# Attention, soft mixture of experts and a Mish layer on one core: the products of probabilities and values in two blocks a pair of heads, and one column block of the folded weights moved ahead of the last layer

## The chip, the cores and the metric

One NeuronCore of one Trainium2 chip runs the program. The metric is device time in microseconds (us) of one execution; the time of a kernel is the median of several runs. Engines: PE is TensorE (PEld its weight loads), DVE VectorE, ACT ScalarE, POOL GpSimd, and SP the queue that issues the DMAs.

## What is computed

```python
# attention: 4 batches, 8 heads, 576 tokens, 64 numbers a head
q_rot, k_rot = rotate(q), rotate(k)
scores = scale * q_rot @ k_rot.T
attn = softmax(scores)                 # over the keys
x = (attn @ v)                         # -> 2304 tokens x 512
# soft mixture of experts, 8 experts of 4 slots
logits = x @ phi                       # 2304 x 32
d = softmax(logits, over tokens); c = softmax(logits, over slots)
slot_out[e] = relu((d.T @ x)[e] @ w1[e]) @ w2[e]
x = c @ slot_out                       # 2304 x 512
# last layer
h = x @ w_in                           # 2304 x 2048
return (h * tanh(softplus(h))) @ w_out # 2304 x 512
```

## The kernel before, in words

**Attention.** The 32 heads are taken as 16 pairs. A pair has nine tiles of scores (128 queries by 576 keys; the ninth holds the last 64 queries of both heads). Each tile goes through four steps: PE multiplies (S, `s_tile`, L333 and L335, or L353 for the ninth), DVE takes the negated row maximum (M, `s_max`, L361), ACT takes the exponential (E, `s_exp`, L367), and PE transposes the 128x128 blocks (T, `t_head`, L374; K, `t_keys`, L388; R, `t_rem`, L394 and L396). ACT or DVE (`evac`, L410 and L413; `t_rem`, L398 to L401) copies the transposed blocks into the tiles PT: group 0 (256 queries: query tiles 0 and 1) and group 1 (320 queries: tiles 2, 3 and the rest).

**Products of probabilities and values.** `av(p, g, c)` (L429) multiplies, for key block c of 0 to 4 and for both heads h, a 128x64 block of values by PT into 64 of the 128 partitions of the PSUM tile `m_av`: head 0 into the lower half, head 1 into the upper half. So a group has ten such products, and a pair has two groups. A product in plain fp32 is two matmul records in the trace. The order in the source is c = 0 head 0, c = 0 head 1, c = 1 head 0 and so on; c = 4 (the last 64 keys, values `vrem`) ends the group, which is then copied out (`xts`) and transposed back (X, `xback`, L449 to L457).

**Order of the work.** The table `PLAN` has one line for each of nine steps of a pair p. A letter is an action, the digit its index, and a "-" behind it means that it is done for pair p - 1. V are the five parts of group 0, W those of group 1. The lines of the table give the order in which the instructions are traced; a scheduler then sets the order of each engine's queue from dependencies and its own model, and may move an instruction ahead of others. `keep_in_program_order` puts an instruction behind the one that was traced before it on its engine. Each engine works through its queue in order.

**Behind the attention** come the routing sums, the experts (L834 and L900, with weights that stream in by DMA), and the last layer. There the product of the slots' outputs with `w_in` is folded: `inner_a(j)` (L981) multiplies the slots' outputs `s_t` with 256 columns of `w_in`, four parts side by side in `m_wp`, and ACT copies them out (L982); `inner_b(j)` (L987) adds the four parts on PE into `m_w`, ACT copies the high part into `wst` (L989) and DVE subtracts to get the low part (L990). `mish(u)` takes unit u (256 tokens, one j): PE makes `hp` from `wst` and the combine weights (L1004), ACT takes Mish (L1011), and the result is split into `gh` and `gl` (L1013, L1019). `second(u)` multiplies both with the parts `wo_h`, `wo_l` of `w_out` into `o_ps` (L1038), 12 products a unit. `parts_of` (L944, L945) and `cv` split `w_out` along the way. `idle(n)` is n products of the identity with itself, whose result is not used (L553). In this part all instructions are pinned to the source's order.

Of the kernel before, what the change touches and what calls it, by code (L numbers as in the profile page):

```python
# [24 lines left out]


PLAN = (
    "L T7- S M K1- E V3- V4-",
    "X0- R- C S M E",
    "S M E W0-",  # L30
    "F T0 r C S M E",
    "S a W1- W2- k F F W3- M T2 T1 E C",
    "S d q C M E",
    "S M C a E T3 W4-",
    "S a C T4 M E",
    "V0 K0 T5 d C F S F M T6 V1 E X1- d V2",
)

EVAC = {"T3": "d", "T4": "d", "K1": "a", "T0": "a", "T5": "a", "T2": "a"}
# [3 lines left out]
def kernel(  # L43
# [13 lines left out]
    nc = tc.nc  # L57
    NB, H, S, D = q.shape
    E, DM, F1 = w1.shape
# [148 lines left out]
    def load_v(p):  # L208
        b, h = divmod(2 * p, H)
        t = vs[p % 3]  # L210
        dma(
            out=t.rearrange("p h c d -> p h (c d)"),
            in_=v[b, h:h + 2, 0:512, :].rearrange("h (p c) d -> p h (c d)", c=4),
        )
        vt[p] = t
# [189 lines left out]
    def evac(dst, src, n, key=None):  # L405

        on = EVAC.get(key) or ("a" if load["a"] <= load["d"] else "d")
        if on == "a":
            load["a"] += n / 1.2 + 50
            nc.scalar.copy(dst, src)  # L410
        else:
            load["d"] += n / 0.96 + 65
            nc.vector.tensor_copy(dst, src)  # L413
# [3 lines left out]
    def av(p, g, c):  # L417
        b, hp = divmod(p, H // 2)
        n = 256 + g * R
        if c == 0:  # L420
            av_ps[p, g] = ps_a.tile([128, n], F32, tag="av", name="m_av")
        ps, pt = av_ps[p, g], PT[p, g]
        for h in range(2):
            o = 64 * h
            if c < 4:
                lhsT, rhs = vt[p][:, h, c, :], pt[:, 5 * h + c, :]
            else:
                lhsT, rhs = vrem[b % 2][:, hp, h, :], pt[:, 4, :]
            nc.tensor.matmul(ps[o:o + 64, :], lhsT=lhsT, rhs=rhs, start=(c == 0), stop=(c == 4))  # L429
        if c == 4:  # L430
            PT.pop((p, g))
            ps = av_ps.pop((p, g))
            xs = a4.tile([128, n], F32, tag="xts", name="xts")
            evac(xs, ps, n, f"X{g}")
            xts[p, g] = xs
            if g and p + 3 < NP:
                load_v(p + 3)
# [111 lines left out]
    def warm(pool, tag, n):  # L549

        ps = pool.tile([128, 128], F32, tag=tag, name="warm")
        for _ in range(n):
            tc.keep_in_program_order(nc.tensor.matmul(ps, lhsT=ident, rhs=ident, start=True, stop=True))  # L553
# [222 lines left out]
    ps = ps_m.tile([128, KDM, NSLOT], F32, tag="m", name="m_sit")  # L776
# [50 lines left out]
    for eg in range(2):  # L827
        for hf in range(2):
            end = eg == 1 and hf == 1
            for fh, cc in [(fh, cc) for fh in range(2) for cc in range(2)]:  # L830
                c = 2 * hf + cc
                for g in range(4):
# [3 lines left out]
                        rhs=parts[1, e, hf][0][:, cc * F1 + fh * 512:cc * F1 + fh * 512 + 512],  # L836
                        start=(eg == 0 and c == 0), stop=(eg == 1 and c == KDM - 1),
# [56 lines left out]
    for eg in range(2):  # L894
        for hf in range(2):
            for cc in range(4):
                c = 4 * hf + cc
                for g in range(4):
# [3 lines left out]
                        rhs=parts[2, e, hf][0][:, cc * DM:(cc + 1) * DM],  # L902
                        start=(eg == 0 and c == 0), stop=(eg == 1 and c == F1 // 128 - 1),
# [8 lines left out]
    ps = ps_m.tile([128, KDM, NSLOT], F32, tag="m", name="m_sot")  # L912
# [28 lines left out]
    def parts_of(c):  # L941

        x = wo_l[c].bitcast(F32)
        pin(nc.scalar.copy(wo_h[c], x))  # L944
        pin(nc.vector.tensor_tensor(out=wo_l[c], in0=x, in1=wo_h[c].bitcast(F32), op=ALU.subtract))  # L945
# [21 lines left out]
    def convert(n):  # L967
        while n:
            x = next(steps2, None)
            if x is None:  # L970
                return
            cv(*x)
            n -= x[1] not in ("S", "H")

    def inner_a(j):

        fb, o = divmod(j * 256, 512)
        wi = parts[3, fb, 0][0].rearrange("p (c f) -> p c f", c=KDM)[:, :, o:o + 256]
        ps = ps_p.tile([128, 256], F32, tag="p", name="m_wp")
        for c in range(KDM):  # L980
            pin(nc.tensor.matmul(ps[32 * c:32 * c + 32, :], lhsT=s_t[:, c, :], rhs=wi[:, c, :], start=True, stop=True))  # L981
        pin(nc.scalar.copy(wps[j % 2], ps))  # L982

    def inner_b(j):

        ps = ps_p.tile([128, 256], F32, tag="p", name="m_w")
        pin(nc.tensor.matmul(ps, lhsT=rr, rhs=wps[j % 2], start=True, stop=True))  # L987
        dst = wst[:, j * 256:(j + 1) * 256]
        pin(nc.scalar.copy(dst, ps))  # L989
        pin(nc.vector.tensor_tensor(out=dst[64:128], in0=ps[64:128], in1=dst[64:128].bitcast(F32), op=ALU.subtract))  # L990
# [3 lines left out]
    NG = NFC // 2  # L994
# [4 lines left out]
    def mish(u):  # L999
        i, j = units[u]  # L1000
        hp = ps_p.tile([128, 2, 256], F32, tag="p", name="hp")
        for x in range(2):
            f = 2 * j + x
            pin(nc.tensor.matmul(hp[:, x, :], lhsT=wst[:, f * 128:(f + 1) * 128],  # L1004
                                 rhs=ct[:, i * 256:(i + 1) * 256],
                                 start=True, stop=True))
        hp = hp.rearrange("p a n -> p (a n)")
        gg = ggs[u % 3]
        gh = p6.tile([128, 512], F32R, tag="gh", name="gh", bufs=LOOK + 1)
        gl = p6.tile([128, 512], F32R, tag="gl", name="gl", bufs=LOOK + 1)  # L1010
        pin(nc.scalar.activation(out=gg, in_=hp, func=AF.Mish))  # L1011

        pin((nc.scalar.copy if 0 < u < NG * GR else nc.vector.tensor_copy)(gh, gg))  # L1013
        gs[u] = gh, gl, gg
# [46 lines left out]
    def idle(n):  # L1061

        warm(ps_o, "o", n)

    inner_a(0)
    parts_of(0)
    idle(3)
    inner_b(0)
    parts_of(1)
    cv(NCE, "S")  # L1070
    idle(6)
    for u in range(len(units) + 2):

        lag = 1 if u < NG * GR else 2
        if u < len(units):
            g, j = units[u][0] // GR, units[u][1]
            i = units[u][0] % GR
            mish(u)
            if u == 0:
                convert(3)  # L1080
                idle(5)
            else:
                if g == 0 or u == NG * GR:
                    rest(u - 1)
                    if u == 1:
                        parts_of(2)
                        parts_of(3)
                    convert(3 + (i == 0))
                if g:
                    rest(u)  # L1090
        else:
            g = None
        if u >= lag and u != NG * GR:
            second(u - lag)
        if g == 0 and i == 2 and j in (0, 2):
            fetch((3, 2 + j // 2, 0), behind=True)
        if g == 0 and j + 1 < NG:

            if i == 0:
                inner_a(j + 1)  # L1100
            elif i == 1:
                inner_b(j + 1)
# [51 lines left out]
```

## Time and profile before

| | us |
|---|---|
| median of 3 runs | 672.29 (671.97 to 673.31) |
| the profiled execution, whole | 671.88 |
| span of its trace | 670.1 |
| attention up to the experts' first product | 0 to 398.8 |
| experts | 398.8 to 434.5 |
| last layer | 434.5 to 670.1 |

The 1.8 us between the whole execution and the span lie around the traced instructions. A row's start is counted from the start of the span. A matmul's end is modelled, so the duration in a row reaches over the start of the next row; what a matmul takes of PE's queue is read from the start of one row to the start of the next.

### The profile page before, as it was taken

What the parts mean: (1) busy time and instruction counts of PE and PEld (TensorE: products, weight loads), DVE (VectorE), ACT (ScalarE), POOL (GpSimd) and SP (SyncE); (2) the same over time, 40 slices, a digit from 0 to 9 for tenths busy, and PEclk for the clock granted to TensorE, in tenths of its full rate; (3) what the DMA queues carried; (4) which work ended last, traced back from release to release, by engine and by line L of the source; (5) the groups of instructions that cost most, each with busy time, mean ns of one, the idle gap of its engine ahead of it and who ended that gap; (6) DMA issues with size and microseconds to landing.
All of it is one profiled execution on the core that took longest, in us unless ns stands there. A gap on an engine that the chain in (4) does not pass through costs nothing.

```text
span 670.1 us, 11089 instructions
## 1 busy us (share of the span) xinstructions
PE 625.2 (93%) x4022; PEld 461.3 (69%) x4022; DVE 406.5 (61%) x824; ACT 336.4 (50%) x757; POOL 218.2 (33%) x263
## 2 busy tenths in 40 slices
PE   1598999989899999999999998999999999999997
PEld 1475677666577767777667653377787888888885
DVE  5777888786686866565756533177876533353342
ACT  2566776684776556665656411167765312222121
POOL 5758869755858644345400010000000000000000
PEclk9999999999999999999999999999999999999999
DMA  9678689868786965346359499962400200030004
GB/s 259 160 187 236 187 268 273 231 212 237 161 266 218 264 184 166 103 128 189 81 176 302 158 338 324 389 262 95 156 33 31 64 1 0 1 95 0 1 1 94
DMA packets 59607, 109.43 MB, mean 163 GB/s; under 512 B 12832, under 2 KB 25248, under 8 KB 59040
## 3 DMA queue, kind: packets, MB, share of 16 engines
q1 hardware_dynamic: 59552, 108.72, 54.2%
q8 instruction: 32, 0.52, 0.3%
q14 instruction: 23, 0.19, 0.1%
HBM read 70.25 MB, written 9.96 MB: 120 GB/s over the span
## 4 chain that ended last, share of the span: by engine, by line
PE 77%; DMA 9%; DVE 7%; ACT 2%; POOL 2%; issue 2%; SPq 1%; DVEq 0%; ACTq 0%; POOLq 0%
PE o_ps L1038 29%; PE m_av L429 13%; PE t L374 7%; PE s L333 5%; PE s L335 4%; PE hp L1004 3%; PE s L353 2%; DMA w<-in_moe_w_in_dram 2%; PE so_ps L900 2%; DMA w<-in_moe_w_dram 2%; DVE nmax L361 1%; PE m_lg L455 1%; PE tk L388 1%; PE m_k L285 1%; DMA w<-in_moe_w_out_dram 1%
## 5 line engine op out<-in xcount | busy, mean ns | idle before, releaser
L361 DVE TENSOR_REDUCE nmax<-s 128x1 f32<-128x576 f32 x144 | 108.0, 753 | 64.3 <-PE s L335 39.5
L367 ACT ACTIVATE P<-s,nmax 128x576 f32<-128x576 f32 x144 | 107.2, 745 | 36.3 <-DVE nmax L361 25.5
L1038 PE MATMUL o_ps<-wo_l,gh 128*128 128x512 f32 x288 | 112.9, 392 | 0.0
L1038 PE MATMUL o_ps<-wo_h,gh 128*128 128x512 f32 x288 | 112.9, 392 | 0.0
L1038 PE MATMUL o_ps<-wo_h,gl 128*128 128x512 f32 x288 | 100.7, 390 | 0.9 <-DVE gl L1019 0.9
L1011 ACT ACTIVATE room<-hp 128x512 f32<-128x512 f32 x72 | 43.0, 599 | 106.7 <-PE hp L1004 102.2
L333 PE MATMUL s<-qk_st 128*128 128x288 f32 x256 | 85.6, 349 | 10.3 <-ACT P L367 5.2
L374 PE MATMUL t<-cs,P 128*128 128x128 f32 x512 | 79.0, 282 | 4.8 <-ACT P L367 2.7
L410 ACT COPY PT<-t 128x512 f32<-128x512 f32 x92 | 53.5, 586 | 49.8 <-PE t L374 49.2
L429 PE MATMUL m_av<-PT,w 128*64 128x320 f32 (+1 forms) x384 | 73.3, 421 | 1.9 <-ACT PT L399 1.3
L374 PEld LDWEIGHTS t<-cs,P 128*128 128x128 f32 x512 | 59.6, 143 | 21.8 <-issue 9.7
L335 PE MATMUL s<-k_st,qk_st 128*128 128x288 f32 x256 | 73.8, 302 | 0.0
L333 PEld LDWEIGHTS s<-qk_st 128*128 128x128 f32 x256 | 49.9, 195 | 29.5 <-ACT P L367 9.1
L1013 DVE CAST gh<-room 128x512 fp32r<-128x512 f32 x49 | 20.9, 427 | 79.4 <-ACT room L1011 79.3
L1038 PEld LDWEIGHTS o_ps<-wo_h,gl 128*128 128x128 f32 x288 | 53.9, 188 | 13.2 <-DVE gl L1019 1.7
L231 POOL TENSOR_TENSOR w<-w,cs 128x512 f32<-128x512 f32 x34 | 45.2, 1332 | 54.1 <-PE m_k L285 46.6
L1038 PEld LDWEIGHTS o_ps<-wo_h,gh 128*128 128x128 f32 x288 | 54.1, 188 | 9.4
L1038 PEld LDWEIGHTS o_ps<-wo_l,gh 128*128 128x128 f32 x288 | 54.3, 189 | 9.0 <-DVE wo_l L891 0.2
L1019 DVE TENSOR_TENSOR gl<-room,gh 128x512 fp32r<-128x512 f32 x72 | 49.6, 691 | 4.6
L335 PEld LDWEIGHTS s<-k_st,qk_st 128*128 128x128 f32 x256 | 50.2, 196 | 0.0
L228 POOL TENSOR_TENSOR w<-w,cs 128x512 f32<-128x512 f32 x34 | 45.7, 1345 | 8.6 <-DMA w<-in_q_dram 2.9
L429 PEld LDWEIGHTS m_av<-PT,w 128*64 128x64 f32 x384 | 26.5, 136 | 23.0 <-issue 9.2
(175 smaller groups left out, 1011.5 us busy)
## 6 DMA issues: line engine op xcount, KB each, us to landing
w<-in_moe_w_dram SPq DMA_DIRECT2D x28, 1024.0 KB, 7.1
w<-in_moe_w_in_dram SPq DMA_DIRECT2D x16, 512.0 KB, 7.3
qk_st<-parth SPq DMA_DIRECT2D x46, 144.0 KB, 3.2
qk_st<-partl SPq DMA_DIRECT2D x46, 144.0 KB, 3.2
room<-in_moe_w_out_dram SPq DMA_DIRECT2D x12, 512.0 KB, 3.6
w<-in_q_dram SPq DMA_DIRECT2D x16, 256.0 KB, 5.2
w<-in_k_dram SPq DMA_DIRECT2D x16, 256.0 KB, 4.6
w<-in_moe_w_dram SPq DMA_DIRECT2D x16, 256.0 KB, 5.6
```

The costliest lines, as they stand in the source:

```text
L228: eng.tensor_tensor(out=tb, in0=src, in1=sin.to_broadcast([128, n, w]), op=ALU.mult)
L231: eng.tensor_tensor(out=dst, in0=sv, in1=cv, op=ALU.mult)
L333: nc.tensor.matmul(s[:, half, 0:288], lhsT=st[:, qc:qc + 128], rhs=st[:, KC + o:KC + o + 288], start=first, stop=False)
L335: nc.tensor.matmul(s[:, half, 0:288], lhsT=st[:, qc:qc + 128], rhs=k2_st[p % 2][:, o:o + 288], start=False, stop=last)
L361: nc.vector.tensor_reduce(out=stat[p][0][:, i:i + 1], in_=s[:, :, 0:288], axis=AX.XY, op=ALU.max, negate=True)
L367: nc.scalar.activation(out=P[p, t][:, h * S:(h + 1) * S].rearrange("p (a b) -> p a b", a=2), in_=s[:, :, 0:288], func=AF.Exp, bias=stat[p] ...
L374: nc.tensor.transpose(ps[:, j, :], P[p, t][:, blk * 128:(blk + 1) * 128], ident)
L410: nc.scalar.copy(dst, src)
L429: nc.tensor.matmul(ps[o:o + 64, :], lhsT=lhsT, rhs=rhs, start=(c == 0), stop=(c == 4))
L1011: pin(nc.scalar.activation(out=gg, in_=hp, func=AF.Mish))
L1019: pin(nc.vector.tensor_tensor(out=gl, in0=gg, in1=gh.bitcast(F32), op=ALU.subtract))
L1038: pin(nc.tensor.matmul(ops[i, n], lhsT=g_[:, cols], rhs=w_[f], start=(j == 0 and (x, k) == (0, 0)), stop=(j == NG - 1 and all(y[0] != n fo ...
```

## The change

All ten products of group 0 (V0 to V4) are traced in step 0 of the next pair, and all ten of group 1 (W0 to W4) in step 4; before, V0 to V2 stood in step 8 of the own pair, and W0 to W4 in steps 2, 4 and 6. Every product but the first of its group is pinned behind the instruction that was traced before it on PE. In the last layer `inner_a(1)` and `inner_b(1)` are moved from inside the first units to the place ahead of the first `mish`, `inner_b(0)` now stands ahead of `parts_of(0)`, and nine `idle` products ahead of the first `hp` become two. The loop makes `inner_a` and `inner_b` for j = 2 to 7.

```diff
@@ -25,15 +25,15 @@
 
 
 PLAN = (
-    "L T7- S M K1- E V3- V4-",
+    "L T7- S M K1- E V0- V1- V2- V3- V4-",
     "X0- R- C S M E",
-    "S M E W0-",
+    "S M E",
     "F T0 r C S M E",
-    "S a W1- W2- k F F W3- M T2 T1 E C",
+    "S a W0- W1- W2- W3- W4- k F F M T2 T1 E C",
     "S d q C M E",
-    "S M C a E T3 W4-",
+    "S M C a E T3",
     "S a C T4 M E",
-    "V0 K0 T5 d C F S F M T6 V1 E X1- d V2",
+    "K0 T5 d C F S F M T6 E X1- d",
 )
 
 EVAC = {"T3": "d", "T4": "d", "K1": "a", "T0": "a", "T5": "a", "T2": "a"}
@@ -426,7 +426,10 @@
                 lhsT, rhs = vt[p][:, h, c, :], pt[:, 5 * h + c, :]
             else:
                 lhsT, rhs = vrem[b % 2][:, hp, h, :], pt[:, 4, :]
-            nc.tensor.matmul(ps[o:o + 64, :], lhsT=lhsT, rhs=rhs, start=(c == 0), stop=(c == 4))
+            mm = nc.tensor.matmul(ps[o:o + 64, :], lhsT=lhsT, rhs=rhs, start=(c == 0), stop=(c == 4))
+            if c or h:
+
+                tc.keep_in_program_order(mm)
         if c == 4:
             PT.pop((p, g))
             ps = av_ps.pop((p, g))
@@ -1063,12 +1066,13 @@
         warm(ps_o, "o", n)
 
     inner_a(0)
+    inner_a(1)
+    inner_b(0)
     parts_of(0)
-    idle(3)
-    inner_b(0)
+    inner_b(1)
     parts_of(1)
     cv(NCE, "S")
-    idle(6)
+    idle(2)
     for u in range(len(units) + 2):
 
         lag = 1 if u < NG * GR else 2
@@ -1094,7 +1098,7 @@
             second(u - lag)
         if g == 0 and i == 2 and j in (0, 2):
             fetch((3, 2 + j // 2, 0), behind=True)
-        if g == 0 and j + 1 < NG:
+        if g == 0 and 0 < j < NG - 1:
 
             if i == 0:
                 inner_a(j + 1)
```

**PE's queue in a pair, group 1 (64x320), before.** S rows are L333 and L335, `t` a transpose, `m_rem` and `m_k` transposes for the next pair.

```order
L374 MATMUL t<-cs,P 128x128 x4
L429 MATMUL m_av<-PT,w_5_1_102 64x320
L333 MATMUL s<-qk_st_123 128x288
L335 MATMUL s<-k_st_121,qk_st_123 128x288
L333 MATMUL s<-qk_st_123 128x288
L335 MATMUL s<-k_st_121,qk_st_123 128x288
L429 MATMUL m_av<-PT,w_5_1_102 64x320
L262 MATMUL m_rem<-cs,w_7_0_100 128x128
L429 MATMUL m_av<-PT,w_5_1_102 64x320 x6
L285 MATMUL m_k<-cs,w_7_0_100 128x128 x4
L429 MATMUL m_av<-PT,w_5_0_98 64x320
L374 MATMUL t<-cs,P 128x128 x4
```

The same place now:

```order
L429 MATMUL m_av<-PT,w_5_1_102 64x320
L333 MATMUL s<-qk_st_123 128x288
L335 MATMUL s<-k_st_121,qk_st_123 128x288
L333 MATMUL s<-qk_st_123 128x288
L335 MATMUL s<-k_st_121,qk_st_123 128x288
L262 MATMUL m_rem<-cs,w_7_0_100 128x128
L429 MATMUL m_av<-PT,w_5_1_102 64x320 x7
L285 MATMUL m_k<-cs,w_7_0_100 128x128 x4
L429 MATMUL m_av<-PT,w_5_0_98 64x320 x2
```

Five runs of products (1, 1, 6, 1 and 1) have become three (1, 7 and 2); the first product of the group still stands alone.

**PE's queue, group 0 (64x256) in the same pair, before.**

```order
L374 MATMUL t<-cs,P 128x128 x8
L429 MATMUL m_av<-PT,v_119 64x256
L333 MATMUL s<-qk_st_123 128x288
L335 MATMUL s<-k_st_121,qk_st_123 128x288
L333 MATMUL s<-qk_st_123 128x288
L335 MATMUL s<-k_st_121,qk_st_123 128x288
L429 MATMUL m_av<-PT,v_119 64x256
L388 MATMUL tk<-cs,P 128x128 x2
L429 MATMUL m_av<-PT,v_119 64x256 x6
```

The same place now:

```order
L374 MATMUL t<-cs,P 128x128 x4
L429 MATMUL m_av<-PT,v_119 64x256
L374 MATMUL t<-cs,P 128x128 x4
L333 MATMUL s<-qk_st_123 128x288
L335 MATMUL s<-k_st_121,qk_st_123 128x288
L333 MATMUL s<-qk_st_123 128x288
L335 MATMUL s<-k_st_121,qk_st_123 128x288
L388 MATMUL tk<-cs,P 128x128 x2
L429 MATMUL m_av<-PT,v_119 64x256 x7
```

Here 1, 1 and 6 have become 1 and 7; the last two (`vrem`) follow some rows later in both. Over the whole queue there are 65 runs of 64x256 before: 34 of one product, 15 of two, 16 of six; now there are 48: 17 of one, 15 of two, 15 of seven, one of eight. Of 64x320 there are 58 before: 23 of one, 19 of two, 12 of six, two of five, one of seven, one of ten; now there are 44: 13 of one, 14 of two, 12 of seven, and one each of three, five, eight, nine and ten.

**PE's queue at the start of the last layer, before.** `warm` are the idle products.

```order
L914 MATMUL m_sot<-cs,si_t 128x32 x4
L981 MATMUL m_wp<-w_0_0_4761,s_t 32x256 x4
L553 MATMUL warm<-cs 128x128 x3
L987 MATMUL m_w<-room,cs 128x256
L553 MATMUL warm<-cs 128x128 x6
L1004 MATMUL hp<-ct,wst 128x256 x2
L553 MATMUL warm<-cs 128x128 x5
L981 MATMUL m_wp<-w_0_0_4761,s_t 32x256 x4
L1004 MATMUL hp<-ct,wst 128x256 x2
L1038 MATMUL o_ps<-wo_h_4882,gh 128x512
```

And now:

```order
L917 MATMUL m_sot<-cs,si_t 128x32 x4
L984 MATMUL m_wp<-w_0_0_4761,s_t 32x256 x8
L990 MATMUL m_w<-room,cs 128x256 x2
L556 MATMUL warm<-cs 128x128 x2
L1007 MATMUL hp<-ct,wst 128x256 x2
L556 MATMUL warm<-cs 128x128 x5
L1007 MATMUL hp<-ct,wst 128x256 x2
L1041 MATMUL o_ps<-wo_h_4882,gh 128x512
```

The second `m_wp` and the second `m_w` stand ahead of the first `hp`; the two first units' `hp` have only idle products between them. The queues of ACT and DVE follow the source in the same way: both copies of `m_wp`, both of `m_w` and both subtractions into `wst` now lie ahead of the first Mish.

## Rows read from the trace of the kernel before

**Rows 1.** Page, part 1 (busy us, share of the span, instructions) and part 5 (groups).

```profile
PE 625.2 (93%) x4022; PEld 461.3 (69%) x4022; DVE 406.5 (61%) x824; ACT 336.4 (50%) x757; POOL 218.2 (33%) x263
...
L410 ACT COPY PT<-t 128x512 f32<-128x512 f32 x92 | 53.5, 586 | 49.8 <-PE t L374 49.2
```

**Rows 2.** Windows: start:end, length, busy (x) of PE, PEld, DVE, ACT, POOL, clock, DMA.

```profile
60.00:100.00 40.00, 38.54 (x272) 27.76 (x272) 32.79 (x65) 26.75 (x64) 32.02 (x36) 1.00 0.80 225
...
140.00:200.00 60.00, 54.26 (x374) 38.76 (x370) 44.19 (x88) 40.62 (x97) 38.72 (x42) 0.97 0.73 209
200.00:392.00 192.00, 188.83 (x1309) 133.86 (x1308) 120.97 (x285) 112.91 (x282) 73.29 (x106) 1.00 0.63 186
```

**Rows 3.** Timeline, PE, pair 1: start, us, engine, line, out<-in, form, count [idle before].

```profile
61.23 0.60 PE L374 MATMUL t<-cs,P 128*128 128x128 f32 x4
61.76 0.65 PE L429 MATMUL m_av<-PT,w 128*64 128x256 f32 x2
62.34 0.66 PE L374 MATMUL t<-cs,P 128*128 128x128 f32 x4
...
64.14 1.51 PE L429 MATMUL m_av<-PT,w 128*64 128x256 f32 x12
65.58 1.09 PE L374 MATMUL t<-cs,P 128*128 128x128 f32 x8
...
66.94 0.65 PE L429 MATMUL m_av<-PT,w 128*64 128x256 f32 x4
67.52 0.66 PE L455 MATMUL m_lg<-phi_sb,xts 128*128 128x64 f32 x4
...
69.00 0.60 PE L374 MATMUL t<-cs,P 128*128 128x128 f32 x4
69.44 0.38 PE L388 MATMUL tk<-cs,P 128*128 128x128 f32 x2
```

**Rows 4.** Timeline, PE, the wider second group of a pair.

```profile
76.28 1.83 PE L429 MATMUL m_av<-PT,w 128*64 128x320 f32 x12
78.05 0.66 PE L285 MATMUL m_k<-cs,w 128*128 128x128 f32 x4
78.64 0.76 PE L429 MATMUL m_av<-PT,w 128*64 128x320 f32 x4
79.33 0.40 PE L333 MATMUL s<-qk_st 128*128 128x288 f32 x1
```

**Rows 5.** Waits of PE, 36 to 392 us: line <- releaser: total, times, longest.

```profile
PE s L353 <- ACT P L367: 3.3, 3, 1.5
...
PE t L374 <- DVE partl L273: 1.9, 1, 1.9
...
PE m_av L429 <- ACT PT L399: 1.3, 1, 1.3
PE m_av L429 <- DVE PT L413: 0.7, 2, 0.5
```

**Rows 6.** Timeline, ACT, start of the last layer.

```profile
440.60 0.58 ACT L1011 ACTIVATE room<-hp 128x512 f32<-128x512 f32 x1
441.96 0.37 ACT L982 COPY room<-m_wp 128x256 f32<-128x256 f32 x1 [0.79 <-PE m_wp L981]
```

**Rows 7.** Timeline, DVE, the same place.

```profile
441.21 0.43 DVE L1013 CAST gh<-room 128x512 fp32r<-128x512 f32 x1 [0.92 <-ACT room L1011]
...
444.17 1.29 DVE L945 TENSOR_TENSOR wo_l<-wo_l,wo_h 128x512 fp32r<-128x512 f32 x2 [0.41 <-ACT wo_h L944]
...
447.35 0.43 DVE L990 TENSOR_TENSOR wst<-m_w,wst 64x256 fp32r<-64x256 f32 x1
447.79 0.69 DVE L1019 TENSOR_TENSOR gl<-room,gh 128x512 fp32r<-128x512 f32 x1
```

**Rows 8.** Timeline, PE, the same place.

```profile
448.53 1.19 PE L1038 MATMUL o_ps<-wo_h,gl 128*128 128x512 f32 x4 [0.93 <-DVE gl L1019]
```

**Rows 9.** Stretch after the longest wait of rows 5, columns as in rows 2.

```profile
147.80:151.10 3.30, 3.30 (x16) 3.29 (x16) 1.98 (x2) 2.14 (x5) 3.30 (x5) 0.50 0.92 242
```


## Prediction

> **What bounds the kernel now.** I read the page first: PE is busy for 93% of the span, its weight loads for 69%, DVE for 61% [rows 1]. Those are averages over stages, so I read the table by stretches next. From 200 to 392 us PE is busy for 188.8 of 192 us, while DVE and ACT have 121 and 113 [rows 2]: here PE's queue sets the pace, and what is taken out of it should come out of the time. From 140 to 200 us PE has 54.3 of 60 us, so almost 6 us are waits for others [rows 2]; from 60 to 140 us it is close to full. The list of PE's waits says who is waited for: the exponentials on ACT (3.3 us, three waits, the longest 1.5), one wait of 1.9 for a subtraction on DVE, and only 2.0 us in the two rows shown of the products themselves waiting for PT [rows 5]. So in the second half of the attention the price is to be read in PE's own queue, from the start of one row to the start of the next, since modelled ends overlap.
>
> **What a run of products costs.** In group 0 (64x256) one product that stands alone (two records) holds the queue from 61.76 to 62.34, 0.58 us [rows 3]. Two products (four records) from 66.94 to 67.52, also 0.58: the halves of the two heads run side by side, and a product without a partner costs what a pair costs. Six products (twelve records) take 64.14 to 65.58, 1.44, so each further pair costs (1.44 - 0.58) / 2 = 0.43. The way in costs something too: four transposes ahead of a product take 61.23 to 61.76, 0.53, but ahead of other transposes 69.00 to 69.44, 0.44 [rows 3], so 0.09 a run. In group 1 (64x320) a pair takes 78.64 to 79.33, 0.69, and six products 76.28 to 78.05, 1.77, so 0.54 for each further pair [rows 4]; for a single one I take the 0.69 of a pair, as in group 0.
>
> **Part 1, the products.** The number of products stays; the number of runs and of products without a partner changes, counted in the queues.
> Group 0 before: 34 single and 15 double runs, 49 x 0.58 = 28.4; 16 of six, 16 x 1.44 = 23.0; 65 ways in, 5.9; together 57.3. Now: 17 single and 15 double, 32 x 0.58 = 18.6; 15 of seven and one of eight, each four pairs, 16 x (0.58 + 3 x 0.43) = 29.9; 48 ways in, 4.3; together 52.8. That is -4.5.
> Group 1 before: 42 short runs x 0.69 = 29.0; 14 of five or six x 1.77 = 24.8; seven and ten 2.31 + 2.85 = 5.2; 58 ways in 5.2; together 64.2. Now: 27 short runs 18.6; twelve of seven and one of eight 13 x 2.31 = 30.0; nine and ten 2 x 2.85 = 5.7; five 1.77; three 1.23; 44 ways in 4.0; together 61.3. That is -2.9, with rounding 7.3 us for both.
>
> The saving is not spread evenly. Counted group by group, the first eight pairs give 1.6 of it (several of their group 1 had already begun with a pair, and now begin with a single one), the last eight 5.7. The last eight lie in the stretch where PE is full, so I take all of the 5.7. The first eight pass through the stretches with other waits [rows 2], so I take half, 0.8; bounds 0 and 1.6.
>
> **What is queued behind the block.** A pinned block is one piece in an in-order queue: if its head waits, the next scores wait too, then the maximum and the exponential. Each block needs the copy of the last transposes, 0.59 us on ACT [rows 1]. In the queue of the pair shown, four other transposes (0.44), four score products and two more transposes stand between those transposes and the block, which covers the copy. But the pins leave the scheduler less freedom than it had. The two waits for PT behind DVE's copy cost 0.7 us in the whole attention before [rows 5]; I charge as much again, +0.7, with bounds of 0 and of the rival below. V0 to V2 come later and W4 earlier: the value tiles are freed and loaded again earlier in the pair, which costs nothing while loads have a whole pair's time; PT of group 0 is held some rows longer, but is first written again in step 3.
>
> **Part 2, the start of the last layer.** PE's last wait is the 0.93 us for the first layer-unit's second `gl` at 448.53 [rows 8]; from there on PE never waits, so the end moves with this `gl`. Two things happen to it. DVE no longer makes the second low part of `wst` right ahead of it: 447.35 to 447.79, -0.44 [rows 7]. Against that, two copies of 0.37 us (as the row at 441.96) stand on ACT ahead of the first Mish, which began at 440.60 [rows 6], so `gh` on DVE starts some 0.7 later than 441.21. DVE then had a wait of 0.41 ahead of 444.17 [rows 7], for casts that ACT now reaches sooner, since the copy at 441.96, with 0.79 of idle ahead of it, no longer stands between the Mishes. So 0.7 - 0.41 - 0.44 gives about -0.2; the bounds are -0.44 (all of the lateness absorbed) and +0.3 (none). PE's own work is lighter here by the seven idle products and by what moves ahead, and will show as longer waits for `gh` and `gl`; that costs nothing by itself.
>
> **Sum.** -5.7 - 0.8 + 0.7 - 0.2 = -6.0 us. The profiled execution took 671.88, so 665.9 by its rows; the median of the runs lies 0.4 above it, and I forecast 672.3 - 6.0 = **666.3 us**.
>
> A rule speaks against counting PE's queue at all: the Trainium skill, page "Perfetto Trace Analysis", section "Identifying the Most-Contended Engine", calls the matmul's busy share a bad measure of how close TensorE is to its limit, and asks for the share of weight loads. This is 133.9 of 192, 70% [rows 2], so by that rule TensorE has room here and the sum would be near 0. I hold against it that the waits listed are few and that starts follow each other at a fixed pace.
>
> **Rivals.**
> *The saving is waited away.* The loop from scores to maximum to exponential to transposes to scores could set the pace, and then a shorter queue only turns into longer waits at S and T. For it: PE waits for ACT's exponentials already [rows 5]. Against it: DVE and ACT are at 63% and 59% from 200 us on [rows 2], and PE's waits there are 3 us in 192. Its time: at most the 1.3 us that can't be told from nothing, 671.0 to 672.3. Chance 0.08. It is the outcome that the cited rule would give.
> *The block waits at its head* (slower). If pinned blocks stand ready in PE's queue before the copy of the last transposes is done, each such wait costs up to the copy's 0.59 us [rows 1]. There are 32 blocks; the saving of 7.3 us is lost from 0.23 us a block on. If every second one waits the whole copy, 16 x 0.59 = 9.4, against 7.3, gives 674.4. For it: the order is set by a model and not by the chip, and before, the scheduler put other work ahead of the second product. Against it: the rows between, above. Chance 0.08.
> *The clock falls.* Behind the wait of 1.9 us [rows 5] the granted clock was 0.50, the 1.2 GHz level, for a stretch of 3.3 us [rows 9], which costs PE about half of that, 1.7 us; behind the waits of up to 1.5 us it was not [rows 5]. With seven idle products fewer, PE will now wait for the first `gh` for around 1 us. If the clock falls there, the forecast becomes 668.0. This lies inside the range and I count it with the forecast.
>
> **Numbers.** The forecast's case has 0.84. A measurement of this kernel can tell about 0.2%, 1.3 us, from no change. The lower end: all of the 7.3, 0.44 at the start of the last layer, and the 2.0 us of waits for PT gone as well make -9.7, 662.6; all of it at once is unlikely, so 663.0. The upper end reaches into the first rival, 671.0. Faster 0.84, within 0.2% 0.08, slower 0.08.
>
> **What would show it.** Right: `m_av` in the profile after falls into some 92 runs, with only about 30 of a single product; PE stays full from 200 us on and the experts begin about 6 us sooner; waits of `m_av` for PT stay under 3 us; in the last layer the wait for `gl` ends some 0.2 us sooner after the experts' end. Wrong: `m_av` or S rows with idle time for PT or P in most pairs (one of the rivals), a PE clock of 0.5 in the last layer, or pairs of the same length as before.

## The result, and the profile after

| | before | after |
|---|---|---|
| median of 4 runs each, same chip | 672.80 (671.97 to 673.54) | 683.54 (676.27 to 688.17) |
| the profiled execution, whole / span | 671.88 / 670.1 | 688.17 / 686.4 |
| the ninth `t4r` of the attention (eight pairs are through) | 231.2 | 247.8 |
| from there to the first `m_sit` (end of the attention) | 166.1 | 166.3 |
| from `m_sit` to the first `m_sot` (experts) | 38.0 | 37.6 |
| from `m_sot` to the end (last layer) | 234.8 | 234.6 |

The change made the kernel slower: ratio 1.0117, 95% interval 1.0078 to 1.0156, where 666.3 us was forecast and 671.0 was the upper end. The ratios here and below are not those of the medians: they leave out runs more than 1.5% above the fastest of their kernel, which count as slow (here 688.17, further down one run of e11). The profiled execution is the slowest of the four, so it shows the loss larger than it is in the median (10.7 us); it lost 16.6 us in the first eight pairs and nothing net anywhere else.

The price of a run of products came out as forecast. The timeline of PE in the kernel after, in a pair that waits for nothing (start, length, line, operation, count):

```profile
273.90 1.03 PE L429 MATMUL m_av<-PT,v 128*64 128x320 f32 x6
274.76 1.51 PE L429 MATMUL m_av<-PT,v 128*64 128x320 f32 x8
276.20 0.66 PE L285 MATMUL m_k<-cs,w 128*128 128x128 f32 x4
...
277.32 0.76 PE L429 MATMUL m_av<-PT,w 128*64 128x320 f32 x4
278.01 1.09 PE L374 MATMUL t<-cs,P 128*128 128x128 f32 x8
...
283.86 1.94 PE L429 MATMUL m_av<-PT,w 128*64 128x256 f32 x14
285.73 0.66 PE L374 MATMUL t<-cs,P 128*128 128x128 f32 x4
...
286.64 0.65 PE L429 MATMUL m_av<-PT,w 128*64 128x256 f32 x4
287.23 0.66 PE L458 MATMUL m_lg<-phi_sb,xts 128*128 128x64 f32 x4
```

From start to start, seven products of 64x320 (one run that two rows of the view share, since a stretch ended between them) hold the queue for 276.20 - 273.90 = 2.30 us (forecast 2.31), a pair for 0.69 (0.69); seven of 64x256 for 1.87 (1.87), a pair for 0.59 (0.58). So the time was not lost in what the change does to these runs. The list of PE's waits says where it was lost. Kernel after, 36 to 409 us, columns as in [rows 5], first six rows and one further:

```profile
PE s L353 <- ACT P L367: 6.3, 3, 3.6
PE s L333 <- DMA qk_st<-parth: 4.8, 2, 3.0
PE t L374 <- DVE partl L273: 3.7, 3, 3.4
PE m_rem L262 <- ACT PT L399: 2.2, 1, 2.2
PE s L333 <- ACT P L367: 2.1, 4, 0.7
PE m_q L285 <- ACT PT L410: 2.0, 1, 2.0
...
PE m_av L429 <- DVE PT L398: 0.5, 1, 0.5
```

The whole list adds up to 29.7 us; the one of [rows 5] adds up to 14.4. The products themselves wait for 0.5. What is new is waits for the stacked keys and queries `qk_st`, which come by DMA (4.8 and 0.6, two rows that had 0.9 together before), and single long waits for operations of ACT and DVE (3.6, 3.4, 2.2, 2.0), where none was longer than 1.9 before.

The table by stretches, cut at the ninth `t4r`, first the kernel before (columns as in [rows 2]):

```profile
0.00:231.20 231.20, 197.28 (x1322) 144.54 (x1323) 175.25 (x339) 146.31 (x340) 166.72 (x185) 0.99 0.80 223
231.20:397.30 166.10, 163.31 (x1141) 114.90 (x1139) 100.26 (x247) 95.06 (x243) 49.78 (x77) 1.00 0.62 186
```

and the kernel after:

```profile
0.00:247.80 247.80, 200.68 (x1322) 150.22 (x1323) 174.35 (x341) 146.42 (x340) 165.12 (x185) 0.96 0.78 216
247.80:414.10 166.30, 161.00 (x1140) 120.09 (x1138) 100.53 (x245) 94.98 (x243) 49.74 (x77) 0.97 0.60 179
```

The work in a row is the same (1,322 matmuls, then 1,140). In the first half PE's idle time went from 231.2 - 197.3 = 33.9 to 47.1 us, and its busy time rose by 3.4 although fewer runs should have lowered it: the mean granted clock fell from 0.99 to 0.96. In the second half the busy time did fall, by 2.3, at a clock of 0.97 and not 1.00, and the idle time grew by 2.5.

### The profile page after: what moved, and what is told of

The parts are those of the page before. It is cut to its first block, busy times and chain, and to the rows that moved or that the text cites. A ratio compares the mean times of both kernels' runs of the same rounds, so it can differ in the third digit from the quotient of the medians.

```text
span 686.4 us, 11068 instructions
## 1 busy us (share of the span) xinstructions
PE 625.3 (91%) x4008; PEld 470.6 (69%) x4008; DVE 405.8 (59%) x824; ACT 336.4 (49%) x757; POOL 216.6 (32%) x263
## 4 chain that ended last, share of the span: by engine, by line
PE 72%; DMA 12%; DVE 6%; ACT 4%; issue 2%; POOL 2%; SPq 1%; DVEq 0%; ACTq 0%; POOLq 0%
PE o_ps L1041 28%; PE m_av L429 10%; DMA w<-in_moe_w_in_dram 6%; PE t L374 6%; PE s L333 4%; PE s L335 3%; PE hp L1007 3%; DMA qk_st<-parth 3%; PE s L353 2%; PE h_ps L837 2%; PE so_ps L903 2%; PE m_lg L458 1%; POOL w L515 1%; ACT P L367 1%; DMA w<-in_moe_w_dram 1%
## 5 line engine op out<-in xcount | busy, mean ns | idle before, releaser
L333 PE MATMUL s<-qk_st 128*128 128x288 f32 x256 | 87.1, 354 | 14.3 <-DMA qk_st<-parth 4.8
L374 PE MATMUL t<-cs,P 128*128 128x128 f32 x512 | 81.0, 288 | 8.1 <-ACT P L367 4.1
L374 PEld LDWEIGHTS t<-cs,P 128*128 128x128 f32 x512 | 61.6, 146 | 24.7 <-issue 11.6
L335 PE MATMUL s<-k_st,qk_st 128*128 128x288 f32 x256 | 75.2, 307 | 0.0
L333 PEld LDWEIGHTS s<-qk_st 128*128 128x128 f32 x256 | 51.1, 200 | 26.7 <-ACT P L367 8.6
L429 PE MATMUL m_av<-PT,w 128*64 128x320 f32 (+1 forms) x384 | 68.6, 424 | 0.0
L1041 PEld LDWEIGHTS o_ps<-wo_h,gh 128*128 128x128 f32 x288 | 54.1, 188 | 10.7 <-DVE gh L1016 1.3
L335 PEld LDWEIGHTS s<-k_st,qk_st 128*128 128x128 f32 x256 | 51.4, 201 | 0.0
L228 POOL TENSOR_TENSOR w<-w,cs 128x512 f32<-128x512 f32 x34 | 45.5, 1338 | 10.2 <-DMA w<-in_k_dram 6.2
L429 PEld LDWEIGHTS m_av<-PT,w 128*64 128x64 f32 x384 | 28.2, 137 | 21.7 <-issue 7.4
```

The lines of the kernel that those rows point to most:

```text
L228: eng.tensor_tensor(out=tb, in0=src, in1=sin.to_broadcast([128, n, w]), op=ALU.mult)
L333: nc.tensor.matmul(s[:, half, 0:288], lhsT=st[:, qc:qc + 128], rhs=st[:, KC + o:KC + o + 288], start=first, stop=False)
L335: nc.tensor.matmul(s[:, half, 0:288], lhsT=st[:, qc:qc + 128], rhs=k2_st[p % 2][:, o:o + 288], start=False, stop=last)
L374: nc.tensor.transpose(ps[:, j, :], P[p, t][:, blk * 128:(blk + 1) * 128], ident)
L429: mm = nc.tensor.matmul(ps[o:o + 64, :], lhsT=lhsT, rhs=rhs, start=(c == 0), stop=(c == 4))
L1041: pin(nc.tensor.matmul(ops[i, n], lhsT=g_[:, cols], rhs=w_[f], start=(j == 0 and (x, k) == (0, 0)), stop=(j == NG - 1 and all(y[0] != n fo ...
```

## The experiments

The unchanged kernel ran beside every experiment; the ratios are to it, with 95% intervals. "First half" and "second half" are the two stretches of the table above, in the profiled execution. From e1 to e4 the kernel before had 673.86 us (19 runs), from e5 to e8 673.51 (7), from e9 to e11 673.37 (19).

| run | median us (n) | ratio | first half | second half |
|---|---|---|---|---|
| after | 683.54 (4) | 1.0117 [1.0078, 1.0156] | 247.8 | 166.3 |
| e1: the last layer's part alone | 673.05 (10) | 0.9984 [0.9961, 1.0007] | 233.6 | 166.1 |
| e2: the new table alone | 680.06 (4) | 1.0100 [1.0039, 1.0162] | 247.3 | 164.7 |
| e3: after, three loads held back | 673.84 (10) | 1.0006 [0.9982, 1.0030] | 242.9 | 160.3 |
| e4: the pins alone | 666.00 (4) | 0.9881 [0.9836, 0.9926] | 231.7 | 162.1 |
| e5: e3, old table for eight pairs, no pins | 665.86 (4) | 0.9891 [0.9846, 0.9936] | 236.0 | 159.7 |
| e6: e5 with the pins | 667.14 (4) | 0.9902 [0.9874, 0.9930] | 232.3 | 161.5 |
| e7: before without 18 loads | 667.09 (4) | 0.9905 [0.9880, 0.9930] | 227.4 | 164.6 |
| e8: e3 without the same loads | 662.70 (4) | 0.9828 [0.9791, 0.9865] | 229.5 | 159.4 |
| e9: e3, conversion's ACT steps pinned | 673.24 (10) | 0.9990 [0.9960, 1.0020] | 239.3 | 164.6 |
| e10: old table, pins, new tail, loads held | 668.72 (5) | 0.9914 [0.9884, 0.9945] | 232.7 | 159.5 |
| e11: e10, conversion's ACT steps pinned | 673.98 (10) | 0.9994 [0.9960, 1.0028] | 241.8 | 160.9 |

### Which part of the change costs the time: e1, e2 and e4

e1 is the kernel before with the last two blocks of the diff (the last layer) alone.

> The kernel before with only the last layer's change (the second inner product of the chain ahead of the first Mish, two idle products for nine). Its attention queues are those of before on every engine. Theory A (all of the loss arises in the attention; the last layer gave what was forecast): from the experts' end to the end of the span 229.5 us against 229.9, the whole 0.2 to 0.5 us below before. Rival (the fewer idle products at the start of the last layer cost something that the profile of the change hides): the same or slower than before by up to 2 us, with a granted clock of 0.5 after 435 us.

Measured 0.9984: no difference that can be told, and in its profile the last layer took 0.4 us less than before, from the first `m_sot` on. The loss is not there.

e2 is the kernel before with nothing but the new table:

```diff
-    "L T7- S M K1- E V3- V4-",
+    "L T7- S M K1- E V0- V1- V2- V3- V4-",
...
```

> The kernel before with only the new table of the attention: no pins on the products, the old last layer. The queues of all engines in the attention are the same as in the changed kernel, so the pins do nothing there. Theory A (the table's new queues make the loss): 0.3 us above the changed kernel, 677 to 688 us, with waits of PE of over 1.5 us in the pairs 0, 2, 4, 5, 7 and 11 and the clock at 0.5 behind them. Rival (the changed kernel's runs were disturbed by the chip): within 2 us of before.

Measured 1.0100, which can't be told from the 1.0117 of the whole change. The order of every engine's instructions in the attention is the same in e2 and in the kernel after: with the new table the pins change nothing. The table is the cause.

e4 is the counterpart, the old table with the pins:

```diff
-            nc.tensor.matmul(ps[o:o + 64, :], lhsT=lhsT, rhs=rhs, start=(c == 0), stop=(c == 4))
+            mm = nc.tensor.matmul(ps[o:o + 64, :], lhsT=lhsT, rhs=rhs, start=(c == 0), stop=(c == 4))
+            if c or h:
+                tc.keep_in_program_order(mm)
```

> The kernel before with the old table and old last layer, and the pins on the products alone: both heads' products of a key block now stand together (124 runs of products, but 5 of a single one against 57). By the price of a run in the rows of before the products take 108.9 us of PE's queue against 121.4. SP's queue keeps the megabyte loads behind the stacking copies. Theory A (fewer lone products pay in full where PE is full, unless queues of loads are disturbed): PE is full from 200 us on, so about 6 us below before in the second half, and between -3 and +3 in the first: 663 to 670. Rival (pinned products wait at the head of PE's queue for PT): as slow as the changed kernel, with waits of the products for PT of over 6 us in all.

Measured 0.9881, 7.9 us faster than before. Here the pins do change the queue: the 65 + 58 runs stay about as many (124), but only 5 of them are a single product, where 57 were.

### The second half: three loads of weights ahead of the stacking copies: e3

PE had two long waits for `qk_st`, of 1.87 us at 243.00, just before the cut between the halves, and of 2.96 us at 332.10, in the second half. The clock was at its lower level behind both. PE's timeline of the kernel after at the longer one (in brackets the idle time and who ended it):

```profile
328.81 0.33 PE L460 MATMUL m_lg<-phi_sb,xts 128*64 128x64 f32 x2
332.10 0.58 PE L333 MATMUL s<-qk_st 128*128 128x288 f32 x1 [2.96 <-DMA qk_st<-parth]
```

SP's timeline says why the copies came late. The kernel after, the head and the end of the twelve stacking copies (L317) of that pair:

```profile
318.54 0.37 SPq L138 DMA_DIRECT2D w<-in_moe_w_dram  x1
319.00 0.47 SPq L317 DMA_DIRECT2D qk_st<-parth  x1
...
322.15 1.36 SPq L317 DMA_DIRECT2D k_st<-parth  x1
...
328.44 0.60 SPq L317 DMA_DIRECT2D qk_st<-partl  x1
```

The same place in the kernel before:

```profile
304.29 0.47 SPq L317 DMA_DIRECT2D qk_st<-parth  x1
...
311.26 0.59 SPq L317 DMA_DIRECT2D qk_st<-partl  x1
311.95 0.55 SPq L138 DMA_DIRECT2D w<-in_moe_w_dram  x1
```

L138 loads 1 MB of the experts' weights. It stood behind the twelve copies and now stands ahead of them; their issues take 328.44 - 319.00 = 9.4 us instead of 7.0, and from issue to landing a copy takes 4.2 to 7.7 us instead of 2.3 to 3.3. The last copy is issued at 328.44, and PE stands still from 332.10 - 2.96 = 329.14 on. The same has happened around 230 us (load at 229.79, wait of 1.87 at 243.00). These loads stand in the source at the end of pair 13 and are not pinned, so the scheduler places them in SP's queue by its own model, and with the new table (e2 has the same order) it places them earlier. e3 holds the three loads of that place to the source's order:

```diff
             for i in (0, 0, 2):
-                fetch(ahead.pop(i))
+                fetch(ahead.pop(i), behind=True)
```

> The changed kernel with the last three megabyte loads of expert weights kept in the order of the source on SP's queue, so that none stands ahead of the copies that stack the next pair's scores operands (in the changed kernel one stands ahead of them at 229.8 and one at 318.5 us). Theory A (those two loads make the waits of 1.9 and 3.0 us at 243 and 332 us, and the falls of the clock behind them): both waits gone, pairs 7 and 11 shorter by about 2.5 and 4.4 us, so some 6 to 7 us below the changed kernel, 676 to 678. Rival (the stacking is late because the products now stand elsewhere): the two waits stay, and the time is that of the changed kernel.

Measured 673.84, 9.7 below the change (6 to 7 were expected): one flag takes back the whole loss. Both waits are gone. SP's order differs from that of the change in these loads alone; the orders of PE, ACT and DVE moved in some places with it. The table by stretches of e3, second half:

```profile
242.90:403.20 160.30, 157.83 (x1141) 117.13 (x1138) 99.97 (x245) 95.04 (x243) 49.75 (x77) 0.99 0.64 197
```

166.1 before, 160.3 now: the -5.7 of the forecast are there as -5.8. What is left is a loss in the first half that eats this gain up: 242.9 against 231.2, in a profiled execution that is e3's slowest (677.21) and so shows it larger than the median does.

### The first half: is it the new table there? e5 and e6

e5 is e3 with the new table from pair 8 on and the old one (`OLD`) before, without pins; e6 adds the pins.

```diff
...
-        for i, step in enumerate(PLAN):
+        for i in range(9):
+            step = (OLD if p < 8 or (p, i) == (8, 0) else PLAN)[i]
...
```

> The changed kernel with the three megabyte loads kept behind (as e3_fetch_late), without the pins, and with the old table for the pairs 0 to 7 and the new table from pair 8 on. SP's queue in the first eight pairs is that of before. Theory A (the second half gives the 5.8 us that e3_fetch_late showed there, the first half loses only through the new queues of loads and conversions): the end of pair 7 at 230 to 233 us as before, and from there to the end as e3_fetch_late: 666 to 668. Rival (the gain of the second half depends on the state that the slow first half leaves, such as weights that have landed by then): the second half loses what the first wins back, 672.

> As e5_mixed_nopin, with the pins on the products: they act where the old table stands, as in e4_pin_only. Theory A: first eight pairs as in e4_pin_only (231.7 us), the rest as in e3_fetch_late (160 to the end of the attention, 37.6, 229.5): 660 to 662, the fastest of all. Rival (the two savings do not add up, since the queues are made anew at the seam): 664 to 668.

Measured 665.86 and 667.14. So, with the three loads held back, the new table gains about 1.1% when it is used in the last eight pairs alone, and loses all of it again when the first eight use it too. The second half of e5, a stretch with no fall of the clock in it:

```profile
236.00:395.70 159.70, 157.08 (x1140) 115.56 (x1138) 98.92 (x246) 95.94 (x244) 49.80 (x77) 1.00 0.65 196
```

PE's busy time is 163.31 - 157.08 = 6.2 us below that of before at the same clock of 1.00. The pins of e6 gained nothing that can be told from e5: the 660 to 662 expected of it were missed, and its rival, 664 to 668, came true.

### The first half: the raw pieces of the last layer's weights: e7 and e8

In the first half 20 pieces of `w_in` and `w_out` (0.5 MB each) are loaded, split into words on ACT (`scale_words`, L503 and L504 of the kernel after) and DVE, summed on POOL and stored. ACT's timeline of the kernel after:

```profile
68.16 0.59 ACT L410 COPY PT<-t 128x512 f32<-128x512 f32 x1
75.48 0.67 ACT L503 ACTIVATE w<-w 128x512 f32<-128x512 f32 x1 [6.73 <-DMA w<-in_moe_w_in_dram]
76.05 0.35 ACT L410 COPY xts<-m_av 128x256 f32<-128x256 f32 x1
```

and SP's, for the piece that it waits for:

```profile
69.98 0.53 SPq L188 DMA_DIRECT2D w<-in_moe_w_in_dram  x1
```

ACT arrived at the conversion before the piece was even asked for, and all its copies and exponentials stood behind it for 6.7 us; the piece landed 5.4 us after its issue. This is the rule that the Trainium skill states on the page "TensorE: Matmul & The Clock Gate", section "Architectural detail: the array is 16× 32×32, not 1× 128×128", that ScalarE takes its instructions strictly first in, first out; the trace agrees, with 6.73 us in which ACT ran nothing. What such a wait costs PE shows further on in the same kernel; ACT first, then PE:

```profile
189.59 0.67 ACT L503 ACTIVATE w<-w 128x512 f32<-128x512 f32 x1 [3.02 <-DMA w<-in_moe_w_out_dram]
...
190.72 0.72 ACT L367 ACTIVATE P<-s,nmax 128x576 f32<-128x576 f32 x1
```

```profile
191.58 0.61 PE L353 MATMUL s<-qk_st 128*128 128x288 f32 x1 [3.60 <-ACT P L367]
```

ACT stood still until a piece had landed, then worked without a gap, and PE stood still until the end of the exponential queued behind the conversion. Of PE's waits of 0.9 us or more in the first half from 36 us on, four in the kernel after follow ACT's waits in this way, 3.60, 2.34, 2.24 and 2.01, together 10.2 us; in the kernel before three do, 1.50, 1.40 and 1.28, together 4.2. The piece at 75.48, behind ACT's longest wait, cost PE little: 0.58 and 0.62. ACT's waits for these pieces in the kernel before (20 to 235 us) are

```profile
ACT w L500 <- DMA w<-in_moe_w_in_dram: 7.5, 7, 2.4
ACT w L500 <- DMA w<-in_moe_w_out_dram: 3.4, 1, 3.4
```

and in e3 (20 to 245 us), where the three loads no longer disturb:

```profile
ACT w L503 <- DMA w<-in_moe_w_in_dram: 15.5, 7, 7.0
ACT w L503 <- DMA w<-in_moe_w_out_dram: 4.3, 2, 3.2
```

10.9 us have become 19.8. e7 is the kernel before and e8 is e3, both without the loads of pieces 2 to 19 (the output is then not the reference's). All other work is done, but the scheduler makes every engine's queue anew, and PE's order too differs in dozens of places:

```diff
-        dma(out=t, in_=src.bitcast(U32))
+        if i < 2:
+            dma(out=t, in_=src.bitcast(U32))
```

> The kernel before, whose conversion of the last layer's weights during the attention works on the first two loaded pieces again and again: 18 of the 20 loads of raw weights are left out, so the folded weights and the output are not the reference's. All the work of ACT, DVE and POOL stays. Theory B (in the first eight pairs ACT's queue stands at the conversion's first step until a piece of raw weights has landed, and exponentials and copies stand behind it): ACT's waits for those loads (10.9 us in the kernel before) are gone and the first eight pairs are 3 to 10 us shorter. Rival (other waits end at the same time anyway): the first eight pairs take 229 to 231 us as before.

> e3_fetch_late with the same 18 loads left out. Theory B: the first eight pairs, 242.9 us in e3_fetch_late, lose all that they have over e7_before_noload, and the kernel is 5 to 7 us below e7_before_noload, as forecast for the change. Rival (the products' new places themselves delay the first eight pairs): it stays some 10 us above e7_before_noload in the first half, and the same or slower in all.

Measured 667.09 and 662.70. Without the raw loads the change as in e3 is worth 4.4 us (5 to 7 were expected), with them 0.0 (e3 against before). The first halves are 227.4 and 229.5, a difference of 2.1 where it was 11.7, so the new table still gains nothing there. PE's list of waits of e8 (36 to 250 us) has as its longest row:

```profile
PE t L374 <- DVE partl L273: 3.1, 1, 3.1
```

This wait is 3.4 in the kernel after and in e3, so the raw loads don't make it; before it was 1.9. So the raw loads are most of what the new table collides with in the first half, and not all. These runs take two things away at once, ACT's wait and 9 MB of traffic on SP's queue, and change the orders besides; the next two try to tell the first two apart.

### Taking ACT's wait away, not the loads: e9 and e11

With the loads in place, both ACT steps of the conversion are held to the source's order, in e9 on top of e3, in e11 on top of e10 (e10 is the old table with the pins, the new start of the last layer and the three loads held back).

```diff
-        nc.scalar.activation(out=hi.bitcast(F32), in_=hi.bitcast(F32), func=AF.Copy, scale=2.0 ** -112)
-        nc.scalar.activation(out=lo.bitcast(F32), in_=lo, func=AF.Copy, scale=2.0 ** -52)
+        for x, e in ((hi, -112), (lo, -52)):
+            tc.keep_in_program_order(
+                nc.scalar.activation(out=x.bitcast(F32), in_=x if e == -52 else x.bitcast(F32), func=AF.Copy, scale=2.0 ** e))
```

> e3_fetch_late with the conversion's two ACT steps pinned to the source's order, so that they stand further behind the load of their piece in ACT's queue; the whole computation is done. Theory B (exponentials stand behind conversions that wait for their load): ACT's waits for raw weights fall from 19.8 us to under 8, the first eight pairs from 242.9 to 230 to 236 us, the whole to 663 to 668. Rival (the pins move the waits to the stacking copies, since SP's queue is made anew): the first eight pairs stay above 240 us and the whole at 672 to 676.

> The old table with the pins on the products (e4_pin_only), the new start of the last layer, and the last three megabyte loads kept behind. Theory A: the gains add up: e4_pin_only less 0.3 us for the last layer; the loads stood well in e4_pin_only, so nothing for them: 664 to 667. Rival (the loads kept behind land too late for the experts, which then wait): the experts' stage over 38.5 us and the whole over 668.

> e10_pin_late_tail with the conversion's ACT steps pinned as in e9_late_cvpin. Theory B: the first eight pairs fall below the 231.7 us of e4_pin_only, to 224 to 230, and the whole to 657 to 664, the fastest of all. Rival (SP's queue, made anew, delays the stacking copies): above e10_pin_late_tail.

Measured 673.24, 668.72 and 673.98. The pins do what they say: ACT no longer waits for a single raw piece between 20 and 245 us in e9 or e11. But no time came back, and in e11 against e10 some 5 us were lost: 663 to 668 and 657 to 664 were expected, and in both the rival's time came true, with its cause, late stacking copies. PE's waits of e9 (36 to 399 us) show the time at another place:

```profile
PE s L333 <- DMA qk_st<-partl: 9.0, 7, 2.6
PE s L333 <- DMA qk_st<-parth: 7.6, 4, 2.6
```

16.6 us for stacking copies, where e3 had 1.6. SP's timeline of e9 ahead of one such wait:

```profile
63.94 0.55 SPq L548 DMA_DIRECT2D scr_in<-w  x1
64.53 0.44 SPq L188 DMA_DIRECT2D w<-in_moe_w_in_dram  x1
65.03 0.50 SPq L317 DMA_DIRECT2D qk_st<-partl  x1
```

and PE's, for the end of the wait:

```profile
71.19 0.40 PE L333 MATMUL s<-qk_st 128*128 128x288 f32 x1 [2.58 <-DMA qk_st<-partl]
```

A store and a raw piece now stand between the last stacking copies, and PE's wait for the last one, issued at 65.03, ends at 71.19, 6.2 us later, where the median of these copies from issue to landing is 3.7 in the same profile. So pinning moved the collision from ACT's queue to SP's. What is shown, by e7 and e8 and by PE's waits behind ACT's: in the first half the raw loads make most of the loss, and taking ACT's wait away alone does not bring it back. What is open: how the loss divides between ACT's wait and the traffic on SP's queue, and an order of SP's queue that serves pieces and copies in time together with the new table; none of these kernels has one, and moving the loads themselves in the source wasn't tried.

e10's second half, 159.5, has no fall of the clock, and its experts took 37.6 us, so the loads held back did not come too late for them, as its rival had it. Its median is not below that of e4 (the intervals overlap; 664 to 667 was expected), so the loads held back gain nothing measurable on top of the old table with pins.

**The best version.** e4, e5, e6 and e10 beat both kernels and can't be told from each other: 0.9 to 1.2% below before, 666 to 669 us. The simplest is e4: the old table, with every product but the first of its group pinned.

## Why the prediction was wrong, point by point

**The price and number of runs: right.** Seven products take 2.30 and 1.87 us, to 0.01 as forecast, and the second half of e3 and e5 gave -5.8 and -6.4 where -5.7 stood. A fall of the clock is in e3's. The rule cited there, of the page "Perfetto Trace Analysis" of the Trainium skill, section "Identifying the Most-Contended Engine", would have had no gain, since weight loads filled 70% of the stretch; in e5 the share is 115.6 / 159.7 = 72% and the gain was had, so here the measurement decides for PE's queue. That section asks for the share of peak arithmetic as well, which was not worked out here.

**The step that failed** is the sum's premise that what is taken out of PE's queue comes out of the time, with the queues of SP and ACT as they were. It shows in one sentence of the part on the block: the value tiles "are freed and loaded again earlier in the pair, which costs nothing while loads have a whole pair's time". It prices the moved loads by their own deadline, and no queue of SP, ACT or POOL was gone through for what a new order of loads pushes aside. Two things came of that, and neither is a load of values. Two 1 MB loads of the experts' weights went ahead of stacking copies, one at the end of the first half and one in the second: 9.7 us on the median (e3). In the first half ACT came to conversions whose raw pieces had not landed, and PE waited behind it (10.2 us in the kernel after, 4.2 before); the old table there gave another 8.0 (e3 to e5). The two come to 17.7, and 16.7 lie between the measured +10.7 and the forecast -6.0. That they meet so closely is partly luck, since these are differences of medians of kernels that scatter by 5 to 12 us.

**The first eight pairs, forecast -0.8 with bounds 0 and -1.6.** Halving the saving allowed for less gain but for no loss, although [rows 2] show 5.7 us of idle PE in one window of 60 and a DMA share of 0.73 to 0.80 there: this stretch waits for transfers, and e3's first half shows that it can get slower when the order changes. Nothing in the rows gave the bound of 0.

**The charge of 0.7 for the pins** was for nothing in this kernel: e2 has the same queues without them. On the old table they are the whole gain of e4.

**The start of the last layer, forecast -0.2.** It came to -0.35 in the profile (229.89 to 229.54 from the first `m_sot` to the start of PE's last instruction). The rows that answer to [rows 6 to 8], in the kernel after; ACT:

```profile
457.76 1.09 ACT L1014 ACTIVATE room<-hp 128x512 f32<-128x512 f32 x2
```

DVE:

```profile
458.39 0.43 DVE L1016 CAST gh<-room 128x512 fp32r<-128x512 f32 x1 [0.54 <-ACT room L1014]
...
463.92 0.68 DVE L1022 TENSOR_TENSOR gl<-room,gh 128x512 fp32r<-128x512 f32 x1
```

PE:

```profile
458.88 0.50 PE L1041 MATMUL o_ps<-wo_h,gh 128*128 128x512 f32 x1 [1.08 <-DVE gh L1016]
...
464.65 1.20 PE L1041 MATMUL o_ps<-wo_h,gl 128*128 128x512 f32 x4 [0.40 <-DVE gl L1022]
```

`gl` ends PE's last wait 464.65 - 451.8 = 12.85 us after the first `m_sot`, before 448.53 - 435.3 = 13.2; the wait for `gh` of "around 1 us" is 1.08. `gh` itself starts 0.7 later than before, counted from there, as forecast.

**The rivals.** "The block waits at its head" has the right sign and the wrong cause: `m_av` waits for PT 0.5 us in all. "The saving is waited away" is e3's total (0.0), but not because the loop of scores and exponentials sets the pace: for the most part by the raw loads. "The clock falls" was right as a mechanism and nearly in price, but looked for in the last layer, where 1.08 us of waiting brought no fall. It came in the attention, mostly behind the new long waits. Of the three none looked at a DMA queue.

## What to carry to other kernels

When a table that a scheduler reads is changed for one engine, the queues of all engines can be made anew (here e2 moved SP's and ACT's): compare each of them, SP's first, and look for a large load that has moved ahead of small copies that someone waits for, and for an in-order engine that reaches a consumer before its load is issued. A stretch whose bounding engine is full can be priced by its own queue; a stretch with idle time and busy transfers can turn either way, and its range has to say so. Where one edit gains in one stage and loses in another, use it in the stage where it gains: half the change (e5), or only its pins (e4), was better than the whole.

## What the runs showed of the hardware that was not expected

**The price of a fall of the clock.** The same 13.5 us of work at the end of the attention, from the last `t4r` to `m_sit`, ran at either level of the clock. The kernel before, and then the kernel after:

```profile
383.80:397.30 13.50, 11.70 (x91) 8.29 (x89) 6.41 (x28) 2.65 (x10) 1.56 (x2) 1.00 1.03 387
```

```profile
399.20:414.10 14.90, 13.19 (x90) 9.89 (x88) 6.38 (x28) 2.65 (x10) 1.52 (x2) 0.89 1.01 376
```

In ten of the thirteen profiles this stretch took 13.5 or 13.6 us; in the other three (after, e3, e4), at a mean clock of 0.89, it took 14.9: 1.4 us a fall. PE's waits in it are the same in both rows' kernels, 0.5, 0.57 and 0.65 us, and the fall came behind the last: the same waits left the clock up in one execution and not in the other. Behind the wait of 2.96 us the fall was twice as long, though behind waits of 3.36 and 3.60 us in the same trace it was not; the stretch in the kernel after:

```profile
331.50:338.40 6.90, 6.30 (x29) 6.27 (x30) 2.89 (x6) 2.66 (x7) 0.32 (x1) 0.51 0.01 5
```

The level is that of 1.2 GHz, and PE had been idle for the 2.96 us right before. In the whole attention the mean clock of the kernel after (0.96 over 247.8 us, 0.97 over 166.3) means about (0.04 x 247.8 + 0.03 x 166.3) x 2 = 30 us at half clock, against the one stretch of 3.3 us of [rows 9] before. A wait of 3 us behind which the clock falls thus costs more than 3 us.

**The scatter.** Kernels whose waits lie at such places scatter: the change from 676 to 688 us, e11 from 669 to 681, the kernel before beside it all from 671 to 677. The mean granted clock, which is on record for every execution, goes with the time: 0.990 at 677.20 and 0.971 at 686.27 us for e2, 0.997 at 669.17 and 0.982 at 676.94 for e11. So of one kernel's executions those with more time at the lower level took longer; whether their waits were longer too isn't known, since only one execution of each was traced.
